# A conditioned transformer layer on one core: c loaded as rows, second FFN in 64-row pairs, another order of work

## The chip, the cores and the metric

The kernel runs on one core of one Trainium2 chip. The metric is the device time of one execution in microseconds (us), lower is better. The core has TensorE (PE, matrix products, with its weight loads), VectorE (DVE), ScalarE (ACT), GpSimd (POOL) and SyncE (SP, which here issues nearly all DMAs). PE writes to PSUM; DVE and ACT read it from there.

## The reference

2048 tokens of width 448, bfloat16. A vector `c` gives six modulation vectors, and two sublayers follow, each behind a layer norm and a modulation:

```python
mod = (_silu(c) @ w_mod).reshape(c.shape[0], 6, 1, -1)
sa, ca, ga, sb, cb, gb = ...
h = _layernorm(x) * (1 + ca) + sa
x = x + ga * _A_ref(h, A_wqkv, A_wo)
h = _layernorm(x) * (1 + cb) + sb
x = x + gb * _B_ref(h, B_w1, B_w2)
```

`_A_ref` is attention with 16 heads of 28, in which token s sees the 8 tokens s, s-2, ..., s-14. `_B_ref` is `silu(h @ w1) @ w2` with an inner width of 1792.

## The kernel before

The tokens are cut into 4 chunks of 512 (k = 0 to 3), each of 4 tiles of 128 tokens. Attention works on 9 blocks (b = 0 to 8) of 112 or 128 positions, even and odd tokens apart (par = 0, 1). The pieces, by the names that stand in the plan:

- `x0a`, `x0b`, `c`, `wm`, `wqk`, `wv`, `x`, `wo`, `w1`, `w2`: loads, all issued on SP but for `c` and `x0b`, which ACT issues. `c` comes in as 112 x 4 values, each on its own.
- `warm`, `junk`: matmuls on zeros ahead of the first real work. `mods`, `gate`: products of Silu(c) with parts of w_mod (L428, L445).
- `n1.k`, `n2.k`: the norms in front of the two sublayers: `stat` on DVE or `sum`, `square` on ACT (L469, L475), `mean`, `rstd`, `nm` on POOL (L472 to L487), `norm` (L494, L496), transposition `T` by DMA (L545; by PE for the first chunk), `mod` on ACT or DVE (L531, L550, L552).
- `QKk.i.g` (L622), `Vb` (L633), `WOk.i` (L748), `F1.k.i` (L786): projections. Their contraction is in part only 64 rows high, so two matmuls on 64 rows each run as a pair in the two halves of PE, into two PSUM banks. Halfway the halves swap banks; between the two parts stands a `turn`: a no-op on POOL (L309) that waits for the last pair and for which the first matmul of the second part waits. Other PE work can be put between.
- `Lb.par` (L665), `expb.par.t` (L673), `mask` (L699), `AVb` (L725), `onorm` (L730, L731), `oTb` (L735): logits, softmax and values. `wo*g`, `wo'`: wo times the gate, and two DMA copies of it within SBUF (L847, L848), for which all of WO waits. `w2*g` (L849): the same for w2.
- `F2.u` (L805): the second FFN matrix, 14 full-height (128-row) matmuls for each 128-token tile, two tiles in one PSUM buffer; `add` (L812) adds x and `st` (L816) stores. The last two tiles are added and stored apart, but share the PSUM buffer.
- `check`, `flag`, `load flag` (L878 to L893): whether all softmax sums are in range; every engine reads the flag before the last store.

PSUM has four buffers of two banks. All these operations are recorded first, with their engines, data dependencies and buffers, and then issued in an order that is written out as a list of numbers (`ORDER`; a trailing `v` or `a` puts an operation on DVE or ACT). Each engine works through its own instructions in that order, and waits where a dependency is not met. If the flag is raised, a slower, safe version of the layer runs behind the first; it does not run here. The numbers in `ORDER` come from a planner that does not run with the kernel, so the nanoseconds given to `P.op` do not touch the written order. ACT needs one table for Exp and another for Silu and loads it at each change between them; Identity, Square and copies run with either.

## Time and profile before

| | us |
|---|---|
| median of 3 runs | 189.16 |
| lowest to highest | 188.3 to 190.1 |
| profiled execution | 187.13 |
| its span | 185.4 |
| PE busy | 167.2 (90%) |
| ACT busy | 112.8 (61%) |
| DVE busy | 94.8 (51%) |
| POOL busy | 27.7 (15%) |

The span runs from the first to the last instruction of one profiled execution, and all durations below come from that. Busy shares are means over the whole span. A busy PE is not PE at its peak: matmuls are pipelined and their ends are modelled, so lengths of runs of matmuls say more than the mean of one.

### The profile page before, as it was taken

How to read it: one execution, taken by the hardware profiler on the slowest of the kernel's cores; microseconds unless marked ns; L12 is line 12 of the kernel's file. 1: busy time of each engine (PE TensorE's matmuls, PEld its weight loads, DVE VectorE, ACT ScalarE, POOL GpSimd, SP SyncE). 2: the span in 40 equal slices, each digit the busy share in tenths (PEclk: the TensorE clock that was granted, in tenths of full speed). 3: DMA queues.
4: the chain of work that ended last, by engine and by line, in shares of the span. 5: the costliest groups of instructions: out<-in, count | busy, mean ns of one | idle time of the engine just before them, and what ended most of it. 6: DMA issues, size and time to landing. Idle time of an engine off the chain costs nothing.

```text
span 185.4 us, 4401 instructions
## 1 busy us (share of the span) xinstructions
PE 167.2 (90%) x1820; PEld 85.6 (46%) x1820; DVE 94.8 (51%) x184; ACT 112.8 (61%) x163; POOL 27.7 (15%) x89
## 2 busy tenths in 40 slices
PE   7589888999938999999999978999979999999960
PEld 2248533554614455444444544565435455444530
DVE  1695968998847298753045953763373102200031
ACT  2077968899637376757978599960339933158000
POOL 2154446202000050013100000122003200000000
PEclk9988999999996699999999999999999999999999
DMA  3999670718999007202020211006620050200021
GB/s 68 295 379 300 145 158 9 162 34 212 305 245 261 0 4 163 53 0 60 0 57 4 48 28 26 4 2 152 160 101 2 4 113 0 101 4 5 2 78 32
DMA packets 32460, 17.49 MB, mean 94 GB/s; under 512 B 24304, under 2 KB 32048, under 8 KB 32432
## 3 DMA queue, kind: packets, MB, share of 16 engines
q1 hardware_dynamic: 31824, 16.90, 35.8%
q8 instruction: 16, 0.26, 0.6%
q10 hardware_dynamic: 608, 0.23, 0.5%
q14 instruction: 12, 0.10, 0.2%
HBM read 9.12 MB, written 1.84 MB: 59 GB/s over the span
## 4 chain that ended last, share of the span: by engine, by line
PE 55%; ACT 17%; DMA 13%; DVE 5%; issue 3%; SPq 3%; POOL 2%; DVEq 0%; ACTq 0%; POOLq 0%
PE ps L786 19%; PE ps L805 17%; PE ps L622 8%; DMA x_all<-in_A_x_dram 6%; ACT p L673 6%; DMA h<-xn 4%; PE ps L633 4%; ACT both L789 3%; PE ps L748 3%; DMA out_dram<-ot 2%; ACT wqk L475 2%; SPq L545 2%; DVE ot L812 1%; PE ps L725 1%; ACT v L637 1%
## 5 line engine op out<-in xcount | busy, mean ns | idle before, releaser
L786 PE MATMUL ps<-h,w 64*128 64x512 bf16 x392 | 44.9, 376 | 1.4 <-DVE ot L812 0.7
L805 PE MATMUL ps<-w,both 128*128 128x448 bf16 x224 | 44.2, 353 | 1.4 <-DVE ot L812 1.4
L789 ACT ACTIVATE both<-ps 128x1024 bf16<-128x1024 f32 x28 | 27.1, 1021 | 16.0 <-PE ps L786 16.0
L673 ACT ACTIVATE p<-ps 128x896 bf16<-128x896 f32 (+1 forms) x36 | 31.2, 937 | 2.6 <-PE ps L665 1.9
L805 PEld LDWEIGHTS <-both 128*128 128x128 bf16 x224 | 21.1, 98 | 22.2 <-issue 3.3
L786 PEld LDWEIGHTS <-w 64*128 64x128 bf16 x392 | 19.9, 94 | 22.9 <-issue 2.5
L812 DVE TENSOR_TENSOR ot<-ps,x_all 128x896 bf16<-128x896 f32 (+1 forms) x9 | 8.8, 986 | 33.2 <-PE ps L805 23.2
L622 PE MATMUL ps<-h,wp 64*128 64x256 bf16 (+1 forms) x224 | 22.6, 344 | 0.2
L699 DVE TENSOR_TENSOR p<-p,maskb 128x1792 bf16<-128x1792 bf16 (+1 forms) x18 | 19.1, 1100 | 3.8 <-ACT p L673 3.8
L622 PEld LDWEIGHTS <-wp 64*128 64x128 bf16 x280 | 14.2, 99 | 11.3 <-issue 1.4
L550 ACT ACTIVATE h<-h,modc 128x512 bf16<-128x512 bf16 x8 | 6.1, 806 | 18.0 <-DMA h<-xn 18.0
L748 PE MATMUL ps<-wo,oT 64*128 64x448 bf16 x112 | 13.9, 372 | 2.5 <-DMA wo<-wo 1.5
L472 POOL TENSOR_SCALAR mv<-sums 128x2 f32<-128x2 f32 x10 | 3.7, 366 | 70.5 <-DVE x_all L763 38.9
L552 DVE TENSOR_SCALAR h<-h,modc 128x512 bf16<-128x512 bf16 x16 | 6.0, 411 | 14.9 <-DMA h<-xn 14.9
L475 ACT ACTIVATE wqk<-x_all,mv 128x448 bf16<-128x448 bf16 x16 | 10.7, 669 | 4.5 <-POOL mv L472 4.3
L496 DVE TENSOR_SCALAR xn<-x_all,mv,rs 128x512 bf16<-128x512 bf16 x26 | 9.8, 416 | 6.3 <-POOL rs L482 6.3
L633 PE MATMUL ps<-wv,h 64*128 64x448 bf16 x98 | 12.8, 382 | 0.1
L763 DVE SCALAR_TENSOR_TENSOR x_all<-ps,x_all 128x448 bf16<-128x448 f32 x16 | 9.3, 621 | 6.5 <-PE ps L748 6.5
L482 POOL TENSOR_TENSOR rs<-rs,negh 128x2 f32<-128x2 f32 x16 | 12.2, 763 | 1.3
L625 DVE CAST qk<-ps 128x512 bf16<-128x512 f32 (+1 forms) x10 | 9.5, 956 | 3.6 <-PE ps L622 3.4
L665 PE MATMUL ps<-qk 28*128 28x112 bf16 (+1 forms) x288 | 7.8, 211 | 2.6 <-ACT p L673 1.1
L465 DVE BATCH_NORM_STATS2 st<-x_all 128x6 f32<-128x448 bf16 x12 | 7.3, 610 | 5.5 <-DMA x_all<-in_A_x_dram 5.5
(76 smaller groups left out, 150.4 us busy)
## 6 DMA issues: line engine op xcount, KB each, us to landing
both<-in_w_mod_dram SPq DMA_DIRECT2D x4, 392.0 KB, 6.6
out_dram<-ot SPq DMA_DIRECT2D x7, 224.0 KB, 2.1
x_all<-in_A_x_dram SPq DMA_DIRECT2D x3, 448.0 KB, 5.9
w<-in_B_w_dram SPq DMA_DIRECT2D x3, 448.0 KB, 5.1
w<-in_B_w_dram SPq DMA_DIRECT2D x1, 896.0 KB, 5.6
both<-in_w_mod_dram SPq DMA_DIRECT2D x1, 784.0 KB, 7.3
w<-in_B_w_dram SPq DMA_DIRECT2D x1, 672.0 KB, 7.7
wqk<-in_A_wqkv_dram SPq DMA_DIRECT2D x1, 448.0 KB, 6.9
```

The source lines that it names most:

```text
L475: S.activation(out=scratch[late], in_=x_all[:, us[j], :], func=ACTF.Square, bias=mv[:, j, 0:1], accum_out=mv[:, j, 1:2])
L482: G.tensor_tensor(out=rs[:, j:j + n], in0=rs[:, j:j + n], in1=negh[:, 0:n], op=ALU.pow)
L496: V.tensor_scalar(out=out_, in0=in_, scalar1=mv[:, j, 0:1], scalar2=rs[:, j:j + 1], op0=ALU.subtract if b else ALU.add, op1=ALU.mult)
L622: return T.matmul(ps[:, j, 0:2 * n], lhsT=w.rearrange("p h d -> p (h d)"), rhs=h[rows, :, t, c0:c0 + n], start=start, stop=stop)
L633: return T.matmul(ps[:, j, 0:D], lhsT=h[rows, j, t, b0:b0 + 128], rhs=wv[rows, t, :], start=start, stop=stop)
L673: S.activation(out=out_, in_=ps[:, :, 0:4 * nq].rearrange("p j (g q) -> p j g q", q=nq), func=ACTF.Exp, scale=SCALE)
L699: V.tensor_tensor(out=p, in0=p, in1=maskb[:, 1 if b == 0 else 0, 0:nq].unsqueeze(1).to_broadcast([128, H, nq]), op=ALU.mult)
L748: return T.matmul(box["ps"][:, j, 0:D], lhsT=oT[rows, j, kk, s0:s0 + 128], rhs=wo[rows, j, kk, :], start=start, stop=stop)
L786: return T.matmul(ps[:, j, :], lhsT=w, rhs=h[rows, :, t, :], start=start, stop=stop)
L789: S.activation(out=hid[:, k % 2, :, i, :], in_=ps[:], func=ACTF.Silu)
L805: T.matmul(box["ps"][:, par, 0:D], lhsT=hid[:, k % 2, f % 2, f // 2, 128 * (2 * i + par):128 * (2 * i + par) + 128], rhs=w2[:, f // 2 + 7 ...
L812: V.tensor_tensor(out=box["o"][:, p0:p1, :], in0=box["ps"][:, p0:p1, 0:D], in1=x_all[:, u + p0:u + p1, :], op=ALU.add)
```

## The change

- `c` is loaded as four rows of 112, goes through Silu in that form, and is turned to columns by a small matmul with the identity (`c T`) and a copy (`scT`).
- The second half of the first tokens (`x0b`) is issued on SP directly behind the first half, ahead of all weights, instead of on ACT. One of six pairs of `junk` matmuls goes.
- The fills of constants, formerly operations of the plan, are all issued in front.
- F2 runs as 64-row pairs with a `turn` between its two parts, except in the last pair of tiles (tokens 1792 to 2047), which keeps full-height matmuls but has one PSUM buffer for each tile.
- The table loads of ACT are issued by name where the table changes.
- `ORDER` is another one. As it stands for each engine: SP has `wo`, `x`, two `wm`, then `wo'` (first), n1.2, one `w1`, `oT0`, `wo'` (second), and the other FFN weights between later transposes; PE has WO0.0, QK2 but its last, AV3, WO0.1, QK2.0.3, V4, V5 and only then QK3; ACT has nine table loads (before: seven), some norms and mods go from ACT to DVE; `check` on PE lies inside the last tile's F2, and both last stores stand behind the flag on SP.

```diff
--- before.py
+++ after.py
@@ -35,7 +35,7 @@
 CP = 256
 BLOCKS = ((0, 1), (2, 3), (4, 5), (6, 7, 8))
 HW = 128 + CP
-WARM, JUNK = 8, 6
+WARM, JUNK = 8, 5
 HOW1 = ("bb", "bbbb", "bbaa", "bbaa")
 HOW2 = ("ssss", "ssss", "ssss", "ssss")
 SEQ = "e0 e1 e2 e3 e4 s0 e5 e6 s1 e7 e8 s2 s3"
@@ -43,28 +43,27 @@
 
 
 ORDER = (
-    "72 0 7 19 20 89 13 88 90 73 21 22 23 24 100 99 25 80 101 11 12 91 26 27 28 29 18 102 36 37 34 35 74 75 76 82 92v 93v 1 81 103v 8 83 94 95 30 31 87a "
...
+    "0 1 71 70 72 73 4 5 2 3 81 9 10 82 6 60 53 61 54 55 56 83 7 8 62a 63 17 18 64 15 16 69v 11 12 84 74v 75v 76 77 85v 86v 87 68a 88 66v 65 79v 13 14 78a "
...
 )
@@ -228,7 +227,12 @@
             seq = [self.ops[i] for i in got]
             for o in seq:
                 o["eng"] = got[o["i"]][1]
+        table = None
         for o in seq:
+            if o["table"] and o["table"] != table:
+                if table:
+                    self.load(o["table"])
+                table = o["table"]
             for r in o["take"]:
                 o["slot"][r] = self.free[self.pool(r)].pop(0)
             o["fn"](o)
@@ -283,7 +287,7 @@
     outb = [ct([128, 2, D], f"ot{i}") for i in range(NO)]
     ident = ct([128, 128], "ident")
     maskb = ct([128, 2, 128], "maskb")
-    cT = ct([RM, KT], "cT")
+    c4, sc4 = (both[0:KT, KT * 6 * D + 1024 + RM * a:KT * 6 * D + 1024 + RM * a + RM] for a in range(2))
     scT = ct([RM, KT], "scT")
     screp = ct([RM, KT, 128], "screp")
     scratch = (both[:, KT * 6 * D + 512:KT * 6 * D + 512 + D], wqk3[:])
@@ -309,11 +313,13 @@
             box["turn"] = G.nop()
             for x in box["last"]:
                 behind(box["turn"], x)
-        return P.op(("pool", 60.0), f, [a], name="turn")
+        return P.op(("pool", 20.0), f, [a], name="turn")
 
     P = Plan()
     for r, n in (("ps", NPS), ("v", NV), ("p", NP), ("xn", NX), ("o", NB2), ("out", NO), ("dma", 8)):
         P.resource(r, n)
+
+    P.load = lambda t: S.preload_act_table(ACTF.Exp if t == "e" else ACTF.Silu)
 
     def copy_on(o):
         return S.copy if o["eng"] == "act" else V.tensor_copy
@@ -337,29 +343,20 @@
     G.memset(epsb[:], EPS)
     G.memset(negh[:], -0.5)
 
...
-    v_ready = fill(vb, lambda t: G.memset(t[:, :, :, DH:32], 1.0), 240.0)
-    p_ready = fill(pb, lambda t: G.memset(t[:, H * 112:H * 112 + 16], 0.0), 60.0)
-    o_ready = fill(ob, lambda t: G.memset(t[:, D:D + 128], 0.0), 160.0)
-    rc_ready = fill((rc,), lambda t: G.memset(t[:], 1.0), 290.0)
-    one_ready = fill((onesf,), lambda t: G.memset(t[:], 1.0), 60.0)
-    wo_ready = [P.op(("pool", 420.0), lambda o: G.memset(wo[half(1), 0, 3, :], 0.0), name="fill")]
+    V.memset(wp[:, :, :, DH:32], 0.0)
+    V.memset(wp3[:, :, DH:32], 0.0)
+    V.memset(wo[half(1), 0, 3, :], 0.0)
+    G.memset(rc[:], 1.0)
+    G.memset(onesf[:], 1.0)
+    for t in pb:
+        G.memset(t[:, H * 112:H * 112 + 16], 0.0)
+    for t in vb:
+        G.memset(t[:, :, :, DH:32], 1.0)
+    G.memset(maskb[:], 1.0)
+    G.affine_select(out=maskb[:], in_=maskb[:], compare_op=ALU.is_ge, fill=0.0, base=-9, pattern=[[16, 2], [-1, 128]], channel_multiplier=1)
+    G.affine_select(out=maskb[:], in_=maskb[:], compare_op=ALU.is_ge, fill=0.0, base=16, pattern=[[-16, 2], [1, 128]], channel_multiplier=-1)
+    for t in ob:
+        G.memset(t[:, D:D + 128], 0.0)
 
 
     def sp(ns, fn, deps, land=0.0, give=(), kb=0.0, run=0, eng="sp", name="dma"):
@@ -378,9 +375,9 @@
 
     ld_x = [[load(224, **first_x(0), run=1792, name="x0a")]]
     first = ld_x[0][0]["deps"][0]
-    ld_c = load(1, cT[:], c.rearrange("o (k p) -> p (o k)", p=RM), run=2, q=nc.scalar, name="c")
-    ld_x[0].append(load(224, **first_x(1), run=1792, q=nc.scalar, after=[ld_c["deps"][0]], name="x0b"))
-    tab = P.op(("act", 1290.0), lambda o: S.preload_act_table(ACTF.Silu), [ld_x[0][1]["deps"][0]], name="table")
+    ld_x[0].append(load(224, after=[first], **first_x(1), run=1792, name="x0b"))
+    ld_c = load(1, c4, c.rearrange("o (k p) -> (o k) p", p=RM), run=224, q=nc.scalar, name="c")
+    tab = P.op(("act", 1290.0), lambda o: S.preload_act_table(ACTF.Silu), [ld_c["deps"][0]], name="table")
 
     def load_mod(c0, c1, after, parts=1):
         n = KT // parts
@@ -405,14 +402,21 @@
     def warm_up(o, n):
         for _ in range(n):
             T.matmul(pst[o["slot"]["ps"]][:, 0, :], lhsT=junk[:, 0:128], rhs=junk, start=True, stop=True)
-    w_last = P.op(("pe", 426.0 * WARM), lambda o: warm_up(o, WARM), take=("ps",), mode="f", name="warm")
+    w_last = P.op(("pe", 216.0 * WARM), lambda o: warm_up(o, WARM), take=("ps",), mode="f", name="warm")
     junks = []
     for _ in range(JUNK):
         junks.append(P.op(("pe", 431.0), lambda o: warm_up(w_last, 2), [w_last] + junks[-1:], mode="f", name="junk"))
     P.op(("none", 0.0), none, junks or [w_last], give=((w_last, "ps"),))
 
 
-    sc_op = P.op(("act", 210.0), lambda o: S.activation(out=scT[:], in_=cT[:], func=ACTF.Silu), [ld_c, tab], table="s", name="silu c")
+    box = {}
+
+    def c_cols(o):
+        box["c"] = bank(o)[0:RM, 0, 0:KT]
+        T.matmul(box["c"], lhsT=sc4, rhs=ident[0:KT, 0:KT], start=True, stop=True)
+    a = P.op(("act", 210.0), lambda o: S.activation(out=sc4, in_=c4, func=ACTF.Silu), [ld_c, tab], table="s", name="silu c")
+    a = P.op(("pe", 60.0), c_cols, [a], take=("ps",), mode="q", name="c T")
+    sc_op = P.op(either(210.0, 75.0), lambda o: copy_on(o)(out=scT[:], in_=box["c"]), [a], give=((a, "ps"),), name="scT")
     rep = P.op(("dve", 310.0), lambda o: V.tensor_copy(out=screp[:], in_=scT[:].unsqueeze(2).to_broadcast([RM, KT, 128])), [sc_op], name="screp")
 
     def mod_cols(vecs, dst0, loads):
@@ -798,40 +802,69 @@
             last = u == 4 * NC - 2
             box = {}
 
-            def part(o, f0, f1, par, i=i, box=box):
-                if f0 == 0 and par == 0:
+            def mm(par, h, f, start, stop, i=i, box=box):
+                rows = half(h)
+                return T.matmul(box["ps"][:, par, 0:D], lhsT=hid[rows, k % 2, f % 2, f // 2, 128 * (2 * i + par):128 * (2 * i + par) + 128],
+                                rhs=w2[rows, f // 2 + 7 * (f % 2), :], start=start, stop=stop)
+
+            def part(o, f0, f1, cross, mm=mm, box=box):
+                if f0 == 0 and not cross:
                     box["ps"] = bank(o)
                 for f in range(f0, f1):
-                    T.matmul(box["ps"][:, par, 0:D], lhsT=hid[:, k % 2, f % 2, f // 2, 128 * (2 * i + par):128 * (2 * i + par) + 128], rhs=w2[:, f // 2 + 7 * (f % 2), :],
+                    x = mm(int(cross), 0, f, f == 0 and not cross, f == NF - 1 and cross)
+                    if cross and f == 0:
+                        behind(x, box["turn"])
+                    y = mm(int(not cross), 1, f, f == 0 and not cross, f == NF - 1 and cross)
+                box["last"] = [x, y]
+
+            def add(o, u=u, box=box):
+                t = box["o"] = outb[o["slot"]["out"]]
+                V.tensor_tensor(out=t[:], in0=box["ps"][:, :, 0:D], in1=x_all[:, u:u + 2, :], op=ALU.add)
+
+            def store(o, u=u, box=box):
+                nc.sync.dma_start(out=out_view[u // 4, u // 2 % 2], in_=box["o"][:].rearrange("p t d -> p (t d)"))
+
+            def whole(o, f0, f1, par, u=u, i=i, box=box):
+                if f0 == 0:
+                    box["ps", par] = bank(o)[:, 0, 0:D]
+                for f in range(f0, f1):
+                    T.matmul(box["ps", par], lhsT=hid[:, k % 2, f % 2, f // 2, 128 * (2 * i + par):128 * (2 * i + par) + 128], rhs=w2[:, f // 2 + 7 * (f % 2), :],
                              start=(f == 0), stop=(f == NF - 1))
 
-            def add(o, pars, u=u, box=box):
-                if "out" in o["slot"]:
+            def add1(o, par, u=u, box=box):
+                if par == 0:
                     box["o"] = outb[o["slot"]["out"]]
-                p0, p1 = pars[0], pars[-1] + 1
-                V.tensor_tensor(out=box["o"][:, p0:p1, :], in0=box["ps"][:, p0:p1, 0:D], in1=x_all[:, u + p0:u + p1, :], op=ALU.add)
-
-            def store(o, pars, u=u, box=box):
-                p0, p1 = pars[0], pars[-1] + 1
-                nc.sync.dma_start(out=out_view[u // 4, u // 2 % 2][:, D * p0:D * p1], in_=box["o"][:, p0:p1, :].rearrange("p t d -> p (t d)"))
-            first, ends = None, []
-            for par in range(2):
-                prev = first
-                for f0, f1 in ((0, 4), (4, 8), (8, 12), (12, 14)):
-                    need = silus[k][f0 // 2:f1 // 2] + w2_gated
-                    prev = P.op(("pe", 189.3 * (f1 - f0)), lambda o, f0=f0, f1=f1, par=par, part=part: part(o, f0, f1, par), need + [prev],
-                                take=("ps",) if first is None else (), mode="f", name=f"F2.{u + par}")
+                V.tensor_tensor(out=box["o"][:, par, :], in0=box["ps", par], in1=x_all[:, u + par, :], op=ALU.add)
+
+            def store1(o, par, u=u, box=box):
+                nc.sync.dma_start(out=out_view[u // 4, u // 2 % 2][:, D * par:D * par + D], in_=box["o"][:, par, :])
+            steps = ((0, 4), (4, 8), (8, 12), (12, 14))
+            if last:
+                ads = []
+                for par in range(2):
+                    prev = None
+                    for f0, f1 in steps:
+                        prev = P.op(("pe", 189.3 * (f1 - f0)), lambda o, f0=f0, f1=f1, par=par, whole=whole: whole(o, f0, f1, par), silus[k][f0 // 2:f1 // 2] + w2_gated + [prev],
+                                    take=("ps",) if f0 == 0 else (), mode="f", name=f"F2.{u + par}")
+                        if f0 == 0:
+                            first = prev
+                    f2_parts.append(prev)
+                    ads.append(P.op(("dve", 541.0), lambda o, par=par, add1=add1: add1(o, par), [prev] + ads, take=() if par else ("out",), give=((first, "ps"),), name=f"add{u}"))
+                    st, a = sp(400.0, lambda o, par=par, store1=store1: store1(o, par), ads[-1:], 1400.0, kb=112.0, run=896, name=f"st{u}")
+                ends_last.extend([ads[-1], a])
+                P.op(("none", 0.0), none, [st], give=((ads[0], "out"),))
+                continue
+            prev, first = None, None
+            for cross in (False, True):
+                wait = [turn(prev, box)] if cross else []
+                for f0, f1 in steps:
+                    need = [] if cross else silus[k][f0 // 2:f1 // 2] + w2_gated
+                    prev = P.op(("pe", 189.3 * (f1 - f0)), lambda o, f0=f0, f1=f1, cross=cross, part=part: part(o, f0, f1, cross), need + [prev] + wait,
+                                take=("ps",) if first is None else (), mode="h", name=f"F2.{u}")
                     first = first or prev
-                f2_read[k].append(prev)
-                ends.append(prev)
-            f2_parts.extend(ends)
-            ads = []
-            for n, pars in enumerate(((0,), (1,)) if last else ((0, 1),)):
-                ad = P.op(("dve", 541.0 if last else 1007.0), lambda o, pars=pars, add=add: add(o, pars), [ends[x] for x in pars] + ads, take=() if n else ("out",), name=f"add{u}")
-                ads.append(ad)
-                st = sp(400.0, lambda o, pars=pars, store=store: store(o, pars), [ad], 1400.0, kb=112.0 * len(pars), run=896 * len(pars), name=f"st{u}")[0]
-            P.op(("none", 0.0), none, ads, give=((first, "ps"),))
-            P.op(("none", 0.0), none, [st], give=((ads[0], "out"),))
+            f2_read[k].append(prev)
+            ad = P.op(("dve", 1007.0), lambda o, add=add: add(o), [prev], take=("out",), give=((first, "ps"),), name=f"add{u}")
+            sp(400.0, lambda o, store=store: store(o), [ad], 1400.0, ((ad, "out"),), kb=224.0, run=1792, name=f"st{u}")
 
     for k in range(NC):
         norm1(k)
@@ -888,12 +921,12 @@
         V.tensor_scalar(out=bad["flag"][:], in0=bad["ps"][0:1, 0, 0:1], scalar1=-1.0, scalar2=float(128 * 2 * NB * H), op0=ALU.mult, op1=ALU.add)
     if not safe:
         ck = P.op(("dve", 1200.0), sums_ok, rc_done + wo_gated + w2_gated, name="check")
-        cm = P.op(("pe", 60.0), sums_all, [ck] + one_ready, take=("ps",), mode="f", name="check")
+        cm = P.op(("pe", 60.0), sums_all, [ck], take=("ps",), mode="f", name="check")
         cf = P.op(("dve", 80.0), sums_bad, [cm], give=((cm, "ps"),), name="flag")
         ld = P.op(("pe", 500.0), lambda o: bad.update(v=nc.values_load(bad["flag"][:], min_val=0, max_val=128 * 2 * NB * H)), [cf] + f2_parts[-1:], mode="f", name="load flag")
-        for o in P.ops:
-            if o["name"] in ("add14", "st14") and o["on"][0][0] in ("dve", "sp") and f2_parts[-1] in o["deps"]:
-                P.need(o, [ld])
+        for o in ends_last:
+            P.need(o, [ld])
+            o["only"] = {"act": ld}
         tc.mark_branch_hint_location("safe", "LikelyTaken")
     P.emit("" if safe else ORDER)
     return bad.get("v")
```

34 lines of the change are left out of this document (10 added, 24 removed), and 41 rows, old and new, of the table ORDER.

## The prediction

> **What bounds the kernel now.** I read the page first: the span, the granted clock and the shares of the chain that ended last.
>
> ```profile
> span 185.4 us, 4401 instructions
> ...
> PEclk9988999999996699999999999999999999999999
> ...
> PE 55%; ACT 17%; DMA 13%; DVE 5%; issue 3%; SPq 3%; POOL 2%; DVEq 0%; ACTq 0%; POOLq 0%
> ```
>
> The chain is mostly TensorE (PE), with DMA and ScalarE (ACT) in it, and in two slices the granted clock falls to 0.6. Where, tell the windows (columns: length, then busy time and instructions of PE, weight loads, VectorE (DVE), ACT and GpSimd (POOL), then clock, DMA share, GB/s):
>
> ```profile
> 13.40:49.10 35.70, 33.46 (x497) 19.09 (x496) 29.32 (x54) 32.07 (x53) 11.55 (x35) 0.97 0.65 162
> 49.10:58.60 9.50, 5.86 (x101) 3.16 (x99) 6.46 (x14) 5.19 (x9) 0.31 (x1) 0.90 1.19 236
> 58.60:62.80 4.20, 4.20 (x22) 1.90 (x24) 1.22 (x2) 0.69 (x1) 0.00 (x0) 0.50 0.39 155
> 49.10:74.90 25.80, 22.16 (x295) 11.62 (x294) 17.45 (x34) 14.18 (x22) 2.98 (x8) 0.87 0.63 142
> 74.90:122.40 47.50, 45.95 (x549) 22.94 (x544) 24.91 (x45) 39.56 (x50) 3.76 (x10) 1.00 0.12 27
> 122.40:137.80 15.40, 14.46 (x122) 7.48 (x121) 7.59 (x16) 3.56 (x7) 2.09 (x6) 1.00 0.40 101
> 137.80:176.50 38.70, 38.67 (x284) 19.00 (x284) 5.90 (x14) 19.03 (x26) 2.71 (x8) 1.00 0.12 37
> ```
>
> From 137.8 to 176.5 us PE never waits; nothing but less PE work helps there. From 49.1 to 74.9 PE waits and runs at a half clock. To see how much is lost I take full-rate durations from the chain in order of time (start, us, what):
>
> ```profile
> 68.30 0.31 PE ps L665 x16
> ...
> 73.06 0.90 PE ps L725 x32
> ...
> 75.58 0.76 PE ps L633 x8
> 76.33 0.76 PE ps L748 x8
> 77.09 0.86 PE ps L786 x8
> ...
> 88.91 2.38 PE ps L805 x12
> ...
> 147.41 10.70 PE ps L805 x56
> 158.11 10.68 PE ps L786 x98
> ```
>
> and the matmul groups of that window:
>
> ```profile
> L622 PE MATMUL ps<-h,wp 64*128 64x512 bf16 x56 | 7.7, 404 | 0.0
> L633 PE MATMUL ps<-wv,h 64*128 64x448 bf16 x42 | 6.2, 424 | 0.1
> L748 PE MATMUL ps<-wo,oT 64*128 64x448 bf16 x28 | 4.4, 437 | 2.0 <-DMA wo<-wo 1.5 <-ACT wqk L475 0.5
> L633 PE MATMUL ps<-wv,wqk 64*128 64x448 bf16 x20 | 2.4, 350 | 0.0
> L725 PE MATMUL ps<-v,p 128*128 128x29 bf16 x67 | 2.2, 176 | 0.0
> L665 PE MATMUL ps<-qk 28*128 28x112 bf16 x48 | 1.1, 210 | 0.0
> L428 PE MATMUL ps<-scT,both 112*128 112x1 bf16 x32 | 0.9, 163 | 1.6 <-ACT v L637 1.6
> ```
>
> At full rate: 56 x 0.109 (98 half-height matmuls of 512 columns, L786, in 10.68) = 6.1; 90 of 448 columns x 0.095 (8 in 0.76) = 8.6; 67 x 0.028 (32 in 0.90) = 1.9; 48 x 0.019 (16 in 0.31) = 0.9; 32 of one column, as many as of 29 in L725, 0.9: 18.4 us of work in 25.8. **7.4 us are lost here**, the largest loss in the span.
>
> **The change part by part.**
>
> *The middle (other order).* PE's two long waits, and what the DMA queue of SP did before them:
>
> ```profile
> 52.83 0.74 PE L748 MATMUL ps<-wo,oT 64*128 64x448 bf16 x6 [1.47 <-DMA wo<-wo]
> ...
> 55.46 0.94 PE L428 MATMUL ps<-scT,both 112*128 112x1 bf16 x32 [1.58 <-ACT v L637]
> ```
>
> ```profile
> 45.02 0.58 SPq L371 DMA_DIRECT2D both<-in_w_mod_dram  x1
> 45.65 0.58 SPq L848 DMA_DIRECT2D wo<-wo  x1
> 46.33 1.50 SPq L545 DMA_TRANSPOSE h<-xn  x1
> 47.88 1.33 SPq L371 DMA_DIRECT2D w<-in_B_w_dram  x1
> ```
>
> The second gated copy of wo, issued at 45.65, is used at 52.83: some 7 us on DMA engines that were full (share 1.19), behind a large w_mod load. The h transpose at 46.33 was as late, so ACT's evacuation of v was late too, and PE waited 1.58. Thin work (5.86 busy in 9.50) was followed by clock 0.50: 22 matmuls that take 22 x 0.1 = 2.2 needed 4.2, another 2.0. Named: 1.47 + 1.58 + 2.0 = 5.05. In the changed program the large w_mod load stands on SP ahead of the first wo copy and the second copy behind oT0 and one w1 load; on PE, three QK2 projections, AV3, WO0.1, the last QK2, V4 and V5 (more than 10 us at the rates above) stand between WO0.0 and the first projection that needs the last h transposes. So the late transfers have cover. Bounds: 7.4 (all of it) and 0 (the loss moves). I take **-4.6**, the named pieces less a tenth, because ACT must keep up: it was busy 32.07 + 14.18 = 46.25 of the 61.5 us from 13.4 to 74.9, and about the same work would sit in 57 (81%), still less dense than the 90% of the stretch to 49.1.
>
> *ScalarE during the first two FFN blocks.* Costs of what is added there:
>
> ```profile
> L673 ACT ACT_TABLE_LOAD x3 | 3.8, 1283 | 0.1
> ...
> L550 ACT ACTIVATE h<-h,modc 128x512 bf16<-128x512 bf16 x8 | 6.1, 806 | 18.0 <-DMA h<-xn 18.0
> ```
>
> The order on ACT alternates Silu and Exp more often: nine table loads instead of seven, and both new ones fall between the first F1.0 Silu and the last F1.1 Silu, with two mods more: 2 x 1.283 + 2 x 0.806 = 4.2 on top of 39.56. Behind them on ACT wait exponentials and Silus, and for these PE. ACT was idle 7.9 us of 47.5, so between 0 and 4.2 shows; I take **+1.6**, nearer the lower end because second FFN work, which does not need ACT at that moment, lies between the phases. Elsewhere ACT gets lighter (norms and mods of the first blocks go to DVE).
>
> *Second FFN as pairs.* Seven of eight pairs of tiles become 28 half-height pairs each: as many slots as the 28 full matmuls. The rows above price both: 56 full ones in 10.70 are 0.191 each, a pair of the same width in L748 is 2 x 0.095 = 0.19. So the pairs themselves: **0** (bounds by these rows: 196 x 0.001 = 0.2 either way). They add seven turns, a POOL no-op for which the second half waits; POOL's own norm steps and later turns queue behind it, and PE behind those. Uncovered, one costs:
>
> ```profile
> 21.05 0.33 PEld L622 LDWEIGHTS <-wp 64*128 64x128 bf16 x8 [0.39 <-POOLq L309]
> ```
>
> 7 x 0.39 = 2.7 at most; I take 0, since in the changed order other PE work of 0.3 us or more stands between the halves each time. Changes of matmul height between neighbours drop from 55 to 51; the 12 matmuls at 88.91 took 2.38 instead of 12 x 0.191 = 2.29, so 0.09 each: **-0.3**.
>
> A page speaks for more: the Trainium skill, "TensorE: Matmul & The Clock Gate", section "Part 3: Packing small matmuls", has weight loads overlap running matmuls only where the row groups differ. By it 196 full-height matmuls would shed an exposed weight load each; this trace disagrees, with 0.191 against 0.19.
>
> *Front.* First rows of x, and c:
>
> ```profile
> 1.24 6.39 DMA x_all<-in_A_x_dram
> ...
> 13.46 4.95 PE ps L622 x68
> ```
>
> ```profile
> 9.03 0.90 PE L428 MATMUL ps<-scT,both 112*128 112x1 bf16 x30 [1.23 <-DMA both<-in_w_mod_dram]
> ...
> cT<-in_c_dram ACTq DMA_DIRECT2D x1, 0.9 KB, 4.0
> ```
>
> The second half of the first tokens took 6.39 us beside the w_mod loads, and the chain runs through it. Now it is second on SP, ahead of them, so its norms can be over when w_mod lands at 9.03, and the mods are shared by ACT and DVE. But the pads and projections still wait for wqk behind the same bytes. I take **-0.5** (between -1.5 and +0.5). c landed after 4.0; its Silu, one small matmul and a copy (each no more than the 0.8 of L550) end before the w_mod load, at 9.03, that the mods need as well: 0, with some 2 us of cover; without it their length, about 1. The fills move ahead of the norms, into the time in which x is under way: 0; what spills over is inside the range of this part.
>
> *Tail.* From the same chain:
>
> ```profile
> 168.79 7.69 PE ps L805 x40
> ...
> 178.23 2.82 PE ps L805 x14
> ```
>
> PE stopped at 176.48 and began the last tile at 178.23: both tiles share one PSUM buffer, and the last one waited for the add of the other. Apart in PSUM this 1.75 goes. Late next would be the flag check, which now lies inside the last tile's 2.8 us with two adds before it; it could give back 0.5. I take **-1.7**. In the window to 137.8 PE idles 15.40 - 14.46 = 0.94; the first stores now stand before the h transposes of that stage instead of among them: **-0.4** (0 to -0.9).
>
> Sum: -0.5 - 4.6 + 1.6 - 0.3 - 0.4 - 1.7 = **-5.9**. The profiled execution took 187.13 (span 185.4), so 181.2 in such an execution. The median of the runs is 189.16, 2.03 above it; on that footing **183.3**.
>
> **The rivals.**
>
> *B, the middle's loss only moves.* ACT and PE are both close to full in the new middle, so PE may wait elsewhere for as long. For it: ACT's 90% before 49.1. Against: that stretch lost little. Without the -4.6: 187.9.
>
> *C, slower: the thin spell comes back at the Exp phases.* Place: between the logits of e5 and the last F1.1 Silu, where ACT switches tables six times. If all 4.2 of its added work reaches PE, that is 2.6 more than I counted, and if PE then falls to the thinness of 49.1 to 58.6 for some 8 us, the clock halves and the loss is that of the middle, 7.4: 183.3 + 2.6 + 7.4 = 193.3. It decides from there: at 62% (5.86 of 9.50) the clock fell, at 97% (74.9 to 122.4) it stayed at 1.00. For it: ACT is 83% busy there already. Against: half of the second FFN fills the gaps.
>
> The Trainium skill's same page, section "Why this matters for your kernels", puts the clock drop at PE-idle gaps above about 3 us. The trace disagrees: 1.47 and 1.58 were the longest here and the clock fell to 0.50. By the page C would end at 185.9.
>
> *D, full-height weight loads are exposed now* and pairs hide them (what the page on packing would make of it). The window from 137.8 has 19.00 us of weight loads in 284, 0.067 each; 196 of these are 13.1: 170.2. The equal rates of full matmuls and pairs deny it.
>
> *E, the pairs don't run side by side.* 196 x 0.191 more: 220.7. L786 and L748 run in pairs now, so hardly.
>
> **How the numbers follow.** Forecast 0.57, B 0.18, C 0.21, D 0.02, E 0.02. A measurement of this kernel tells about 1% from no change, 187.3 to 191.1. Faster: 0.57 + 0.02 + 0.03 of B = 0.62; same: 0.15; slower: 0.21 + 0.02 = 0.23. The forecast's own range, with its terms not all at one end, is 180 to 187. The whole range reaches over B to C: 179.5 to 193.5.
>
> **What would show it.** Right: no 0.6 in the clock row after the first slices; the wo copy landed before WO0.0; PE's wait before the last tile gone, the last tile directly after the one before; F2 pairs at 0.19; the first F1 matmul at about 70 us instead of 74.9. Wrong: ACT idle on PE and PE on ACT in turn between table loads, PE waits on POOL turns, or a new DMA wait of several us before the first FFN.

## The result, and the profile after

| | before | after |
|---|---|---|
| median of the runs | 188.73 us (185.87 to 190.1, 4 runs) | 174.52 us (174.0 to 175.33, 4 runs) |
| profiled execution | 187.13 us, span 185.4 | 174.45 us, span 172.6 |

The changed kernel takes 0.933 of the time (95% interval 0.921 to 0.945), 14.2 us less in the medians, 12.7 in the profiled executions. Some executions of the kernel before are slower at a lower clock, so this ratio and those below compare only the faster executions of both kernels (of the kernel before 185.87 and 188.3 us here) and show less gain than the medians. The forecast was 5.9 us less. The page of the kernel after, the same rows as shown of before:

```profile
span 172.6 us, 4801 instructions
...
PEclk9987999999999999999999999999999999999999
...
PE 82%; DVE 5%; DMA 3%; ACT 3%; SPq 2%; issue 1%; DVEq 0%; ACTq 0%
```

The fall of the granted clock in the middle is gone, and 82% of the chain is PE instead of 55%. The windows of the kernel after, cut at the same points of the work (first queries, about the old 49.1, first FFN begins, first FFN of chunk 1 over, late stage over):

```profile
13.30:43.80 30.50, 28.96 (x502) 18.06 (x503) 28.28 (x56) 27.44 (x43) 9.03 (x21) 0.97 0.77 182
43.80:63.60 19.80, 19.80 (x264) 10.58 (x265) 18.93 (x40) 16.31 (x28) 4.67 (x12) 1.00 0.75 141
63.60:111.80 48.20, 48.10 (x662) 24.54 (x658) 29.14 (x48) 42.68 (x55) 5.68 (x15) 1.00 0.34 51
111.80:125.60 13.80, 13.80 (x148) 6.98 (x146) 5.08 (x13) 6.28 (x12) 1.64 (x6) 1.00 0.51 90
125.60:165.70 40.10, 40.10 (x378) 19.18 (x374) 8.79 (x16) 13.69 (x14) 1.09 (x3) 1.00 0.14 43
```

From 43.8 to 165.7 us PE waits 0.10 us in all, at full clock. Set beside the windows of before, the time that PE did not work or worked at half rate went from 2.24 to 1.54 before the middle (-0.7), from 7.4 to 0 in the middle, from 1.55 to 0.10 in the first FFN blocks, from 0.94 to 0 in the late stage. The tail, in the chain in order of time:

```profile
13.34 5.57 PE ps L626 x82
...
150.86 10.59 PE ps L807 x112
161.45 4.27 PE ps L831 x22
165.72 0.12 PE ps L917 x2
165.84 1.26 PE ps L831 x6
...
167.12 0.62 DVE ot L837
```

The first queries begin at 13.34 instead of 13.46 (-0.1); the last two tiles follow each other without the old 1.75 us (-1.75). These add up to 0.7 + 7.4 + 1.45 + 0.94 + 0.1 + 1.75 = 12.3. The last matmul ends 13.95 us earlier (181.05 to 167.10), so some 1.6 is not in these waits: fewer changes of matmul height and pairs at 10.59 / 56 = 0.189 instead of 0.191 are part of it, the rest I can't place. From the end of the last addition (167.74) to the end of the span it is 4.86 us, before 3.70 (181.70 to 185.4), so 1.2 is given back there.

### The profile page after: what moved, and what is told of

Its sections match the earlier page's. It is cut to its first block, busy times and chain, and to the rows that moved or that the text cites. A ratio compares the mean times of both kernels' runs of the same rounds, so it can differ in the third digit from the quotient of the medians.

```text
span 172.6 us, 4801 instructions
## 1 busy us (share of the span) xinstructions
PE 161.4 (94%) x2015; PEld 83.9 (49%) x2015; DVE 98.0 (57%) x196; ACT 110.1 (64%) x155; POOL 28.1 (16%) x88
## 4 chain that ended last, share of the span: by engine, by line
PE 82%; DVE 5%; DMA 3%; ACT 3%; SPq 2%; issue 1%; DVEq 0%; ACTq 0%
PE ps L790 24%; PE ps L807 22%; PE ps L626 14%; PE ps L752 7%; PE ps L637 6%; PE ps L729 4%; DMA wqk<-in_A_wqkv_dram 3%; PE ps L831 3%; PE ps L669 3%; ACT p L677 2%; SPq L368 2%; DVE p L703 1%; DVE xn L500 1%; ACT L322 1%; DVE v L641 1%
## 5 line engine op out<-in xcount | busy, mean ns | idle before, releaser
L790 PE MATMUL ps<-h,w 64*128 64x512 bf16 x392 | 45.1, 376 | 0.0
L807 PE MATMUL ps<-w,both 64*128 64x448 bf16 x392 | 40.4, 349 | 0.0
L790 PEld LDWEIGHTS <-w 64*128 64x128 bf16 x392 | 19.5, 94 | 22.0
L807 PEld LDWEIGHTS <-both 64*128 64x128 bf16 x392 | 18.6, 94 | 17.9
L822 DVE TENSOR_TENSOR ot<-ps,x_all 128x896 bf16<-128x896 f32 x7 | 7.5, 1090 | 28.0 <-PE ps L807 27.9
L626 PE MATMUL ps<-h,wp 64*128 64x256 bf16 (+1 forms) x224 | 21.9, 333 | 0.3
L500 DVE TENSOR_SCALAR xn<-x_all,mv,rs 128x512 bf16<-128x512 bf16 x29 | 10.9, 406 | 3.9 <-POOL rs L486 3.7
L629 ACT CAST qk<-ps 128x1024 bf16<-128x1024 f32 (+1 forms) x11 | 9.3, 859 | 2.7 <-PE ps L626 2.6
L637 PE MATMUL ps<-wv,h 64*128 64x448 bf16 x98 | 10.8, 350 | 0.0
L735 DVE TENSOR_TENSOR o<-ps,rc 112x896 bf16<-112x896 f32 (+1 forms) x9 | 9.8, 1091 | 0.3
L556 DVE TENSOR_SCALAR h<-h,modc 128x512 bf16<-128x512 bf16 x19 | 6.7, 407 | 5.2 <-DMA h<-xn 5.2
L729 PEld LDWEIGHTS <-p 128*128 128x128 bf16 x288 | 7.7, 96 | 3.5 <-issue 1.5
```

The costliest lines, as they stand in the source:

```text
L500: V.tensor_scalar(out=out_, in0=in_, scalar1=mv[:, j, 0:1], scalar2=rs[:, j:j + 1], op0=ALU.subtract if b else ALU.add, op1=ALU.mult)
L626: return T.matmul(ps[:, j, 0:2 * n], lhsT=w.rearrange("p h d -> p (h d)"), rhs=h[rows, :, t, c0:c0 + n], start=start, stop=stop)
L637: return T.matmul(ps[:, j, 0:D], lhsT=h[rows, j, t, b0:b0 + 128], rhs=wv[rows, t, :], start=start, stop=stop)
L729: T.matmul(box["ps"][:, par, h, 0:DH + 1], lhsT=p[:, at:at + 128], rhs=v[:, h, 0:DH + 1], start=True, stop=True)
L790: return T.matmul(ps[:, j, :], lhsT=w, rhs=h[rows, :, t, :], start=start, stop=stop)
L807: return T.matmul(box["ps"][:, par, 0:D], lhsT=hid[rows, k % 2, f % 2, f // 2, 128 * (2 * i + par):128 * (2 * i + par) + 128], rhs=w2[rows ...
```

## Experiments

Theory: the gain is that of the other order, whose middle no longer waits for late transfers. Rival: the other parts (pairs, fills, rows of c, PSUM) carry it. "Tile 1" to "tile 3" in the expectations are the chunks 1 to 3 of 512 tokens. The comparisons ran on several chips; the kernel before had medians of 186.3 to 188.7 us in these comparisons, the kernel after 174.5, 174.9 and 174.3.

**1. The old code in the new order.**

```diff
-ORDER = (the order of before)
+ORDER = (the order of after, entry for entry, the fills in front)
```

> The kernel before in every instruction (c element by element, x0b on ACT's queue, second FFN at full height, last two tiles in one PSUM buffer), written out in the order of the kernel after, the fills in front as there. If the order carries the gain: the kernel after plus the shared buffer of the last tile (1.75 us) plus at most 1 us for pairs, mode switches and the front, so 176 to 177.5 us, ratio 0.935 to 0.94, and no slice of the granted clock under 0.97 after 20 us. If the other parts carry it: 184 us or more, ratio over 0.975.

Measured: 177.97 us (177.63 to 178.3), ratio 0.963 (0.955 to 0.971), a little slower than expected. The order alone carries more than half of the gain: 3.7% of 6.7% by the ratios, about three quarters by the medians (3.5 us of 14.2 are missing). From 37 us to the first FFN its timeline of PE is that of the kernel after within 0.1 us (first matmul of the first FFN at 63.60; after: 63.50); then it falls 3 us behind. Two rows of it:

```profile
153.66 14.93 PE L805 MATMUL ps<-w,both 128*128 128x448 bf16 x78
...
169.36 1.29 PE L805 MATMUL ps<-w,both 128*128 128x448 bf16 x6 [0.65 <-DVE flag L888]
```

The last run of second-FFN matmuls starts at 153.66, in the kernel after at 150.86. PE's wait in the last tile is 0.65 in this order, not 1.75; the row puts it down to the flag on DVE, which stands behind the addition that reads that tile's PSUM buffer, so whether the shared buffer makes it is not shown.

**2. The new code in the old order.**

```diff
-ORDER = (the order of after)
+ORDER = (the order of before; c's matmul and copy behind its Silu; swapped halves behind the straight ones)
```

> The counterpart: the instructions of the kernel after (rows of c, x0b on SP, pairs in the second FFN with the swapped halves just behind the straight ones, last two tiles apart, fills in front) in the order of the kernel before. If the order carries the gain: only the tail and under 1 us of the rest, so 185.5 to 187 us, ratio 0.983 to 0.99, and the stretch of 49 to 61 us still with PE idle and a granted clock under 0.8. If the other parts carry it: 177 to 180 us.

Measured: 187.39 us (187.0 to 188.17), ratio 1.013 (1.003 to 1.023). Without the order the parts bring nothing, less than I expected; so the part of the gain that the order alone does not bring (3.0 of 6.7%) comes only with order and parts together. The waits of PE in it:

```profile
PE ps L669 <- DVE v L641: 2.7, 1, 2.7
...
PE ps L432 <- ACT v L641: 1.6, 1, 1.6
PE ps L752 <- DMA wo<-wo: 1.2, 1, 1.2
```

The old middle is there (the last two rows), and the wait for an eviction of v by DVE at 27 us, 0.74 in the kernel before, has become 2.71. The tail of PE is shorter here too (last matmul over at 179.64 instead of 181.05), but from the last addition to the end it takes 5.65 us instead of 3.70.

**3. The old kernel with another order on SP alone.**

```diff
 (SP, the other engines as they were)
+x of chunk 3, 784 KB of w_mod
 transposes of chunk 1
-x of chunk 3
 ... first transpose of oT
+second copy of wo, transposes of chunk 3
 112 KB of w1, 896 KB of w2
-transposes of chunk 3, 784 KB of w_mod, second copy of wo
```

> The kernel before with only SP's order changed, the other engines' streams row for row as they were: x of tile 3 and the 784 KB of w_mod ahead of the transposes of tile 1, the second copy of wo right behind the first transpose of oT, the 112 KB of w1 and the 896 KB of w2 behind the transposes of tile 3. If late transfers are the cause of the lost time between 20 and 62 us (5.39 us on x of tile 3, 7.38 us on the transposes of tile 3, 1.47 us on the copy of wo, and the clock after them): 5 to 8 us faster, ratio 0.955 to 0.975, no granted clock under 0.9 at 49 to 62 us. If the streams of PE, ACT and DVE are the cause and the transfers merely end last: under 2 us, ratio over 0.99.

Measured: 194.77 us (193.53 to 195.23), ratio 1.051 (1.040 to 1.062): slower, where one theory had it faster and the other unchanged. What DVE waited for (total, times, longest):

```profile
DVE w L849 <- DMA w<-in_B_w_dram: 6.3, 1, 6.3
DVE h L552 <- DMA h<-xn: 5.4, 1, 5.4
```

Transfers moved ahead of the transposes of chunk 1 made these late (5.4), and w2, moved back, was now late for its scaling on DVE (6.3), with everything behind it on DVE's queue. The place of a transfer is right or wrong only against the queue that consumes it.

**4. The new kernel with the old order on SP.**

```diff
 (SP, behind the first transpose of oT)
+112 KB of w1, 896 KB of w2, 784 KB of w_mod
 second copy of wo, 672 KB of w2, 112 KB of w1
 ... (the three added loads go from their places: w_mod from far ahead, w1 and w2 from behind)
```

> The kernel after with SP's order made like the old one behind the first transpose of oT: 112 KB of w1, 896 KB of w2, the 784 KB of w_mod and only then the second copy of wo; all other engines as they were. If late transfers are the cause by themselves: 3 to 7 us slower than the kernel after (178 to 181.5 us, ratio 0.95 to 0.97), with PE idle before the first matmul of wo or of the first FFN and a fall of the granted clock. If the new streams of PE cover late transfers: within 1 us of 174.5.

Measured: 183.92 us (183.19 to 185.21, 10 runs), 9.4 us above the kernel after and 0.995 (0.990 to 0.999) of the kernel before: nearly all of the gain is gone, more than either expectation had. PE's wait in it, and its clock:

```profile
PE ps L432 <- DMA both<-in_w_mod_dram: 7.8, 1, 7.8
```

```profile
44.00:49.00 5.00, 1.98 (x68) 1.80 (x69) 0.89 (x4) 0.44 (x1) 0.00 (x0) 0.50 1.06 286
```

PE's cover of the new order doesn't help: its mods stand in its queue at 39 us and wait for w_mod 7.8 us, and half clock follows. The load that does it here is the 784 KB of w_mod, issued at 38.94 us instead of 23.93; the copy of wo didn't show. So 1, 3 and 4 together: the new streams gain with their own SP order and lose nearly all of it with an order like the old one, and the old streams lost with the SP order of experiment 3, which is like the new one only in part.

**5. The two waits that the prediction named, taken away in the old kernel.** First the copy of wo alone:

```diff
 (SP) first transpose of oT
+second copy of wo
 w1, w2, first transpose of chunk 3, 784 KB of w_mod
-second copy of wo
```

> The kernel before with only the second copy of wo moved on SP, from behind w1, w2, the first transposes of tile 3 and the 784 KB of w_mod to right behind the first transpose of oT. The prediction's named piece: PE's wait of 1.47 us on this copy goes, and with it a part of the half clock behind it: 1.5 to 3 us faster. If DVE's wait on the transposes of tile 3 (2.46 us to 53.82, with the additions to x behind it) sets the stretch: under 0.7 us.

Measured: 186.08 us (185.0 to 189.32, 10 runs), ratio 0.997 (0.992 to 1.002): nothing. The wait on the copy is gone from PE's timeline, another has grown from 1.58 to 3.40:

```profile
54.27 0.99 PE L428 MATMUL ps<-scT,both 112*128 112x1 bf16 x32 [3.40 <-ACT v L637]
```

ACT is late with v because the modulation of h stands ahead of it in ACT's queue and waits there, as the kernel before shows:

```profile
53.80 0.81 ACT L550 ACTIVATE h<-h,modc 128x512 bf16<-128x512 bf16 x1 [4.31 <-DMA h<-xn]
```

So next the modulations of h were moved back, with the copy of wo late as it was and early:

```diff
 (ACT) -modulate h of chunk 3 / evict v / exp / +modulate h of chunk 3
 (DVE) -two of its parts / two additions to x / +the two parts
```

> The kernel before with three instructions moved down their queues and nothing else: on ACT the modulation of h of tile 3 (it stood 4.31 us for the transposes, until 53.80) behind one eviction of V and one exponential, on DVE its two counterparts (2.46 us) behind the two additions to x. If what was lost at 49 to 56 us is ACT standing at a late transpose with V's eviction behind it: PE's 1.58 us on that eviction go, but its 1.47 us on the copy of wo stay: 1 to 2 us faster. If PE meets the modulated h itself next: within 0.5 us.

Measured: 186.76 us (186.04 to 189.97, 11 runs), ratio 1.003 (0.998 to 1.008): nothing.

> The kernel before with the same three instructions moved, and SP's second copy of wo right behind the first transpose of oT. Both named waits of the stretch are taken away (3.40 us on V's eviction where only the copy was moved). If these two waits are the loss that the prediction counted (3.05 us, and 2.0 at half clock behind them): 3 to 5 us faster, clock at 1.0 from 49 to 62 us. If further waits of the old order come up in their place: under 1.5 us.

Measured: 186.67 us (184.33 to 189.88, 4 runs) beside 186.58 of the kernel before. Both named waits are gone, and the medians are the same. The ratio, from only two executions of this kernel (184.33 and 185.43 beside a mean of 186.0), is 0.994: a gain of about 1 us may be there, but not the 3 to 5 us expected if these waits were the loss. In their place (timeline of PE, then a window):

```profile
56.99 1.68 PE L748 MATMUL ps<-wo,oT 64*128 64x448 bf16 x8 [2.88 <-DMA oT<-o]
```

```profile
55.00:61.00 6.00, 4.01 (x22) 1.91 (x24) 1.40 (x2) 0.97 (x3) 0.00 (x0) 0.50 0.64 207
```

The transposes of oT, issued on SP behind the same loads, are now last, and the half clock is there as before. Taking the two waits away does not take the loss away; another transfer of that time ends last instead.

**6. The burst.** Windows of the kernel before, then after, for the DMA share (second column from the end):

```profile
26.00:32.00 6.00, 4.80 (x66) 2.28 (x67) 5.13 (x13) 4.01 (x7) 2.67 (x7) 1.00 0.06 20
...
44.00:49.00 5.00, 5.00 (x108) 3.04 (x104) 4.33 (x6) 5.00 (x7) 0.36 (x3) 1.00 1.07 307
49.00:55.00 6.00, 3.41 (x51) 1.73 (x48) 3.50 (x6) 1.69 (x3) 0.00 (x0) 1.00 1.18 255
```

```profile
26.00:32.00 6.00, 6.00 (x72) 2.73 (x70) 5.31 (x12) 5.27 (x10) 2.62 (x5) 1.00 0.81 216
...
44.00:49.00 5.00, 5.00 (x66) 2.79 (x63) 5.00 (x11) 4.18 (x10) 1.41 (x4) 1.00 0.81 105
49.00:55.00 6.00, 6.00 (x81) 3.02 (x81) 5.45 (x13) 4.46 (x8) 1.46 (x4) 1.00 0.67 139
```

The old order leaves the DMA engines nearly idle at 26 to 32 us and fills them from 44 to 55, when transposes and copies are needed; the new one spreads the same bytes. Only one load was moved, in the old kernel:

```diff
 (SP) transposes of chunk 2
+784 KB of w_mod
 first transpose of oT, w1, w2, first transpose of chunk 3
-784 KB of w_mod
 second copy of wo
```

> The kernel before with only the 784 KB of w_mod moved on SP, from behind the first transpose of tile 3 to behind the transposes of tile 2. If the burst is the cause, taking 0.78 of its 1.8 MB out gives a part: 1.5 to 4 us faster. If not: within 1 us.

Measured: 182.71 us (181.38 to 183.7), ratio 0.983 (0.975 to 0.992); the kernel before had 186.44 beside it. One load, moved by 11 us, gives some 3 us (1.5 to 4.7 by the interval); in the profiled execution (span 179.7) the first matmul of the first FFN stands at 68.93 instead of 74.77, and the granted clock has no fall:

```profile
PEclk9978999999999999999999999999999999999999
```

```profile
52.00 0.94 PE L428 MATMUL ps<-scT,both 112*128 112x1 bf16 x32 [0.77 <-ACT v L637]
55.16 0.93 PE L748 MATMUL ps<-wo,oT 64*128 64x448 bf16 x8 [1.08 <-ACT wqk L475]
68.93 0.81 PE L786 MATMUL ps<-h,w 64*128 64x512 bf16 x6
```

The wait on v is halved, that on the copy of wo gone. The transposes of chunk 3 land after 5.6 us in the median of two instead of 7.4, the second copy of wo after 5.7 instead of 7.1. But the DMA engines are as full from 44 to 55 us as they were:

```profile
44.00:49.00 5.00, 5.00 (x110) 3.21 (x108) 4.33 (x7) 4.50 (x6) 0.00 (x0) 1.00 1.25 252
49.00:55.00 6.00, 4.22 (x92) 2.47 (x86) 5.46 (x13) 4.65 (x8) 0.31 (x1) 1.00 1.13 249
```

So what went is the wait behind this load, not the full engines. The whole burst spread by hand:

```diff
 (SP) x of chunk 3
+896 KB of w2, 112 KB of w1
 first copy of wo, transposes of chunk 2
+784 KB of w_mod
 first transpose of oT
+second copy of wo
 transposes of chunk 3
```

> The kernel before with only SP's order changed, other streams row for row as they were: the 896 KB of w2 and 112 KB of w1 right behind x of tile 3 (into 24 to 32 us, where the DMA engines' share is 0.06 to 0.2), the 784 KB of w_mod behind the transposes of tile 2 (34 to 40 us), and then only the first transpose of oT, the second copy of wo and the transposes of tile 3, which meet empty queues. If the burst of 1.8 MB at 41 to 47 us (DMA share 1.07 to 1.18 until 55 us) is what the old order loses its middle to: the waits at 49 to 61 us and the half clock go, 4 to 7 us faster, ratio 0.96 to 0.98. If the streams of PE, ACT and DVE have no work to put there anyway: under 1.5 us.

Measured: 185.24 us (182.99 to 188.39), ratio 0.986 (0.979 to 0.992): some gain, below the expectation and by the ratios no more than that of the smaller edit. Its profiled execution (187.4 us) has a new loss earlier:

```profile
27.77 0.55 PE L665 MATMUL ps<-qk 28*128 28x112 bf16 x14 [2.85 <-DVE v L637]
```

This wait is 0.74 in the kernel before, and the clock from 26 to 32 us is 0.56 instead of 1.00; a transpose of chunk 1 stands on SP just ahead of the added loads and took 5.5 us instead of 3.4. How much of this stands in its other executions is not shown. So that the burst as a whole is the cause is argued; what is shown is the effect of the one load.

**7. Pairs, in the new order.**

```diff
-x = mm(int(cross), 0, f, ...); y = mm(int(not cross), 1, f, ...)
+x = T.matmul(ps[:, par, 0:D], lhsT=hid[:, ...], rhs=w2[:, ...], start=(f == 0), stop=(f == NF - 1))
```

> The kernel after with only the second FFN back at full height (128-row weights, one tile whole and then the other, in the same order of the queue; no swapped halves that wait on a turn). As the prediction has it, pairs are worth 0 and a change of the matmul form 0.09 us: 24 more changes (75 against 51) give at most 2.2, and the pairs themselves nothing, so 174.5 to 176.7 us. If pairs are what lets this order change between the two FFNs for nothing: the 2.9 us that the run of the old code in the new order lost between 66 and 151 us, so 177 to 178 us.

Measured: 177.21 us (176.35 to 178.23): 2.7 us slower than the kernel after. Its chain in order of time shows where:

```profile
149.25 1.62 PE ps L815 x8
150.87 0.97 PE ps L790 x8
151.84 0.48 PE ps L815 x2
152.33 0.97 PE ps L790 x8
153.30 10.70 PE ps L815 x56
```

A long run of full-height matmuls (56 in 10.70) is as fast as pairs; each change between the two heights costs some 0.1 (8 matmuls of L790 in 0.97, in the kernel after in 0.86; 2 of L815 in 0.48 instead of 0.38). Up to the last long run it is 2.4 us later than the kernel after (153.30 against 150.86), although its first FFN began 0.33 earlier (63.17 against 63.50): 2.77 in 24 more changes (26 by the records of the two traces), 0.11 to 0.12 each. Pairs are worth nothing alone and 2.7 us in this order, which changes often between the two FFNs.

**8. More work for ACT, new order and old.**

```diff
+n-th change of table in (2, 5, 7), old kernel (2, 3, 4): one more ACT_TABLE_LOAD of the other table
```

> The kernel after with three more ACT_TABLE_LOADs (the other table, and then the right one, at the second, fifth and seventh change of table; 3 x 1.283 = 3.85 us more work on ACT, between 64 and 93 us). By the prediction's share of added ACT work that comes through (about 0.4): 1.5 us slower, 176 us. If PE's queue in the new order has so much work ahead of what waits for ACT that it is covered: within 0.4 us of the kernel after, 174.1 to 174.9 us. If ACT bounds this stretch in the new order: the whole 3.85, 178.4 us.

> The kernel before with three more ACT_TABLE_LOADs at its second, third and fourth change of table (76 to 102 us, 3.85 us of ACT). By the prediction's share 0.4: 1.5 us slower. If in the old order, too, ACT's work in the FFN blocks comes through nearly whole (0.92 in the new order): 3.5 us slower.

Measured in the new order: 178.06 us (177.93 to 179.28), 3.5 us slower than the kernel after, nearly all of the 3.85. PE now waits where it did not:

```profile
67.59 0.37 PE L676 MATMUL ps<-qk 28*128 28x112 bf16 x14 [0.57 <-ACT both L800]
...
96.43 0.93 PE L759 MATMUL ps<-wo,oT 64*128 64x448 bf16 x8 [1.05 <-ACT p L684]
```

In the old order: 186.52 us (184.74 to 190.01, 10 runs), ratio 1.000 (0.996 to 1.005): nothing, where both expectations had it slower. Neither run shows the share of 0.4 of the prediction. In the old order ACT stands idle before the instructions behind these loads, and a load fills that time: of 0.71 us ahead of a Silu and 1.15 ahead of an exponential, 0 and 0.43 are left. The new order needs ACT just in time.

**9. More junk in front.**

```diff
-for _ in range(JUNK): warm_up(w_last, 2)
+for n in (2, 2, 11, 2, 2): warm_up(w_last, n)
```

> The kernel after with nine more 128x512 matmuls on zeros in the third batch of junk (11 in place of 2), which fill PE's idle time from 6.35 to 8.3 us (2.54 us idle until 8.90 in the kernel after). If that idle time is what halves the granted clock at 11.7 to 14.5 us: clock 1.0 there, and the first queries' matmuls 0.7 us faster; if the stretch of 20 to 38 us, where DVE is busy 5.96 of 6 us, takes this back, 0 to 0.2 us at the end (174.3 to 174.6), else 0.7 us (173.8). If the clock falls for another reason: no change of the clock, 174.5 us.

Measured: 175.89 us (174.94 to 176.31), slower than expected. The kernel after, unchanged, on another chip:

> The kernel after, unchanged, on one chip with these three, to see how far its 174.5 us hold from chip to chip: 174 to 175.5 us. If 176 comes out, the run with more junk did not lose 1.4 us, and if 174.5, it did.

Measured: 174.91 us (174.2 to 177.09), ratio 0.940 (0.931 to 0.949). So more junk brings no gain, if not a loss of up to 1 us. The clock did rise; the same window of the kernel after, then of this one:

```profile
13.30:20.00 6.70, 6.66 (x98) 5.46 (x100) 5.62 (x15) 5.04 (x12) 2.63 (x8) 0.88 0.30 67
```

```profile
13.30:20.00 6.70, 6.39 (x106) 5.24 (x108) 5.73 (x16) 5.04 (x12) 2.63 (x8) 1.00 0.30 68
```

But PE now waits for the modulated h within the first queries (1.02 us in three waits, two of them here), and the matmuls behind these queries start at 18.62 instead of 18.73:

```profile
12.78 0.28 PE L626 MATMUL ps<-h,wp 64*128 64x256 bf16 x2 [0.67 <-ACT h L535]
13.24 1.18 PE L626 MATMUL ps<-h,wp 64*128 64x256 bf16 x13 [0.17 <-ACT h L535]
```

At 34 us, where DVE is busy 5.96 of 6 us, PE waits 1.14 us for DVE's mask instead of 0.72, and the 0.1 is gone.

**10. The end.**

```diff
 (SP)
+first store of the last two tiles
 load of the flag
-first store of the last two tiles
 last store
```

> The kernel after with one instruction moved on SP: the first store of the last pair of tiles (112 KB, its sum is ready at 165.68) ahead of the load of the flag, as the kernel before has it, instead of behind it (issued at 166.95, some 0.8 us ahead of the last store). In the kernel after, 4.86 us pass from the end of the last addition (167.74) to the end of the span, in the kernel before 3.70 (181.70 to 185.4), and the two stores take 3.0 us to land instead of 1.8. If the two stores hinder each other: 0.5 to 1.1 us faster than the kernel after beside it. If the flag's way through SP sets the end: within 0.3 us.

> The kernel after, unchanged, on the same chip as the run with the store moved, as its measure: 174 to 175.5 us.

Measured: 174.36 us (173.78 to 176.8, 6 runs) beside 174.32 (174.08 to 174.81, 6 runs). The stores land in 2.2 instead of 3.0 us, and the end does not move. What lengthened the end by 1.2 us stays open. None of these versions beats the kernel after.

## Why the prediction was right and wrong

The direction was right, and in the middle the mechanism too (other order, late transfers, clock); the size was half, and the term for ACT had the wrong sign. In the profiled executions 12.7 us went instead of 5.9. Of the 6.8 between, 3.05 are the ACT term and 2.8 the middle: these two are the steps that failed. The rest is made of smaller terms, some of them the other way.

- **The middle, -4.6: measured -7.4, and 0.7 more ahead of it.** The step: "Named: 1.47 + 1.58 + 2.0 = 5.05 ... I take -4.6, the named pieces less a tenth". The loss is not a sum of such waits: with both taken away (experiment 5) at most about 1 us was gained, as a third, 2.88 us, took their place. They stand behind the same loads; one load moved (experiment 6) gave some 3 us without any change in the queues of PE, ACT and DVE. In the changed kernel the whole 7.4, the bound that I worked out and set aside, is gone. How it divides between the loads and PE's new cover is not shown. ACT, for which I had made the term smaller, was busy 27.44 + 16.31 = 43.75 of 50.3 us (87%; I had worked out 81%) and kept up.
- **ACT in the first FFN blocks, +1.6: measured -1.45, a wrong sign.** The added work is there: seven table loads instead of five, and ACT busy 42.68 of 48.20 us instead of 39.56 of 47.50. But PE waits 0.10 us. The step: I let a fixed share of 0.4 of added ACT work come through to PE. Experiment 8 has 0 in the old order and 0.92 in the new one: the share belongs to the order, not to the stage. The old stretch had 1.55 us of PE waiting to lose, which I had left in it.
- **Late stage, -0.4: measured -0.94,** the end of its bounds; no experiment took it apart.
- **Tail, -1.7: PE's 1.75 went, 1.2 came back** after the last addition. I had allowed for 0.5, at the flag.
- **Pairs 0, changes of height -0.3, turns 0:** right as to rates (0.189 and 0.191) and as to the price (0.09 worked out, 0.11 to 0.12 measured). What I did not see is what pairs are worth in this order: without them it has 75 changes instead of 51 and takes 2.7 us more.
- **Front, -0.5: -0.1,** inside its bounds. A full clock there would not have helped (experiment 9): PE then waits for the modulated h.
- **The footing, +2.03:** I lifted the sum by what lay between the profiled execution of before and the median. The kernel before spreads from 183.9 to 190.1 us over these comparisons, the kernel after mostly within 1 us of 174.5, and its profiled execution lies at the median. Without the lift the forecast would have been 181.2.

None of the rivals came. B (the loss only moves) is what experiment 5 shows for single edits in the old order, but not for the change; C did not come, as the clock of the profiled execution never fell after the front; D and E are denied by 56 full matmuls in 10.70 beside 56 pairs in 10.59.

## What to carry to other kernels

Before summing the waits of a bad stretch, look for what they share: here waits on a copy, on an eviction behind late transposes, and on other transposes stood behind the same large loads and replaced each other, and moving one load helped. The DMA share by windows (0.06, and then 1.18) shows where to look, but is not the cause by itself: with the load moved it was as high. An order over several in-order queues is best seen as one: two larger rearrangements of SP's queue alone cost 5%, while one load moved alone gained 2%. And a price measured in one order (ACT work at 0.4, pairs at 0) isn't the price in another.

## What the runs showed of the hardware that was not expected

The granted clock halved after an idle time of 2.54 us: in the kernel after PE stands from 6.35 to 8.90, and the clock is 0.75 and then 0.50 from 11 to 14 us. With most of that time filled by matmuls on zeros (experiment 9) it stayed at 1.00.

```profile
8.90 0.95 PE L432 MATMUL ps<-scT,both 112*128 112x1 bf16 x32 [2.54 <-DMA both<-in_w_mod_dram]
```

```profile
11.00:12.00 1.00, 1.00 (x8) 0.54 (x8) 0.89 (x5) 0.24 (x1) 0.00 (x0) 0.75 1.06 378
12.00:13.00 1.00, 0.90 (x4) 0.20 (x3) 0.47 (x2) 0.73 (x2) 0.00 (x0) 0.50 1.07 370
```

By the Trainium skill, "TensorE: Matmul & The Clock Gate", section "Why this matters for your kernels", it takes a gap above about 3 us; here 2.54 was enough.

A transpose between SBUF tiles takes 2.8 us from issue to landing in the median of the kernel before (its list of DMA issues), and in its chain one of chunk 3 took 7.38, issued behind 0.9 MB of w2 and 0.78 MB of w_mod:

```profile
h<-xn SPq DMA_TRANSPOSE x12, 2.8
```

```profile
46.33 7.38 DMA h<-xn
```
